# Attention, mixture of experts and gated FFN on one core: token counts one unit later, the last group's factors inside the FFN stage, the silu table loaded early

## The chip, the cores and the metric

One core of a Trainium2 chip runs the whole program. The metric is device microseconds of one launch; the kernel before took 783.86 us, the median of three runs (782.74 to 785.09). One more execution was taken by the profiler; the rows further down are from it.

## The reference, cut to what matters

Three stages follow each other on 2304 tokens of width 512.

```
attention: q, k, v of (4 batches, 8 heads, 576, 64), 128 random features
  phi(x) = exp(h - max h) / sqrt(128),  h = x_s @ omega.T - |x_s|^2 / 2
  out = phi(q) @ (phi(k).T @ v) / (phi(q) . sum phi(k) + 1e-6)
experts (8, 512 -> 1024 -> 512): each token goes to the expert with the
  largest cosine to its embedding
  out[token] = gate * (relu(x @ w1[e]) @ w2[e])
ffn (512 -> 1536 -> 512):
  out = (silu(x @ w_gate) * (x @ w_val)) @ w_out
```

All inputs and outputs are float32.

## The kernel before, in words

**Precision.** A large product is made of three passes: an operand is split into a high part (a cast on ScalarE, line 92) and a low part (the rest, a subtraction on VectorE or GpSimd, line 93), and high x high, high x low and low x high are summed in PSUM. The helper `hi_lo` writes both parts.

**Attention.** Tokens go in 18 tiles of 128, in two groups of nine. The order of this stage is written by hand. Behind each group a class `Routing` works out logits, softmax, the chosen expert of each token, the gate values, and per batch of 576 tokens how many tokens chose each expert. `counts` sums the one-hot rows over the partitions by a small matmul with ones (line 327), turns the gate values by a transpose (line 331), copies them out on ScalarE (line 333) and stores them by a DMA. Then VectorE finds the expert that most tokens of a batch chose (`dom_i`), the counts of the others (`ext_i`) and their total (`tot_i`, line 351), which all engines load into a register (line 1001) for the branch of line 988.

**Experts.** For each batch `expert` runs the dominant expert on all its tokens: four units of hidden columns (`mm1`, 48 matmuls of 288 columns each: two halves of 128 hidden columns, 24 each), then four output chunks (`mm2`, 48 each). The other experts' tokens follow in the branch "extras". Weights of a unit come by a DMA and `hi_lo`; the first two units' low parts are made on GpSimd. For the third unit of the first expert both instructions of `hi_lo` are pinned (`pinned="both"`, lines 94 to 97). PSUM holds two tiles `two` and one tile `third` for these products; a ReLU on ScalarE (line 888) and a subtraction on VectorE (line 889) empty a tile. After the fourth unit `no_y` writes zeros over the output sums `y_g` with 12 ScalarE copies (line 1009). Hooks, keyed by batch and step, put other work between the units: `routing_end` (rest of `Routing` for the second group) stands behind the first unit of the first expert.

**FFN.** Products of 2x2 blocks are done with seven multiplications in place of eight (`PRODUCTS`), so the tokens' activations need seven factors for each of three groups of 768 tokens. `split_y` writes them from `y_g`: `put` is a `hi_lo`, `sub` a subtraction on VectorE (line 965). The last group's `split_y` begins behind the last expert's third output chunk and the rest of it is written at the end of the expert stage. Then, for 12 column blocks and three groups, `tokens` does the seven products (line 1109), empties `a`, `b`, `c` in PSUM (lines 1074 to 1099), applies silu (line 1077), and stores the hidden block to DRAM. `beside` puts the weights' conversion and their seven factors (`seven`) between the products. `out_ahead` fetches a pair of output weight blocks with two DMAs and converts them from 64-bit words (`words`: one ScalarE and six VectorE instructions, the first two pinned). The last stage multiplies hidden blocks by output weights (line 1180).

**What sets the order.** Outside attention, a planner at build time orders each engine's instructions. It takes an instruction when its costs say that its operands are there, and of several the one traced first. `keep_in_program_order` pins an instruction behind the one that was traced just before it on its engine; later ones may still pass it.

Of the kernel before, what the change touches and what calls it, by code (L numbers as in the profile page):

```python
# [10 lines left out]
F32 = mybir.dt.float32  # L11
# [3 lines left out]
AF = mybir.ActivationFunctionType  # L15
# [13 lines left out]
def attention_moe_ffn_kernel(  # L29
# [4 lines left out]
    nc = tc.nc  # L34
# [8 lines left out]
    NF = w64.shape[0]  # L43
# [185 lines left out]
    class Routing:  # L229
# [94 lines left out]
        def counts(self):  # L324
            g = self.g
            p = bank(2, E)
            nc.tensor.matmul(p, ones, self.oc, start=True, stop=True)
            cnt = self.small("cnt", 2, E)
            nc.vector.tensor_copy(cnt, p)
            p = bank(128)  # L330
            nc.tensor.transpose(p[:PT * E, :], self.gt.rearrange("p i e -> p (i e)"), ident)
            gt_t = rt.tile([PT * E, 128], F32, name="gt_t")
            nc.scalar.copy(gt_t, p[:PT * E, :])
            nc.sync.dma_start(out=gts[g], in_=gt_t)
            yield
            cm = self.small("cm", 2)
            dom = self.small("dom", 2, E)
            fst = first_max(cm, dom, cnt, 2, "c")
            nc.vector.tensor_copy(dom_i[:, 2 * g:2 * g + 2], fst[0:1, :])
            yield  # L340
            nc.vector.scalar_tensor_tensor(
                out=cnt, in0=dom, scalar=0.5, in1=cnt, op0=ALU.is_lt, op1=ALU.mult
            )
            c1 = cnt[0:1].rearrange("p j e -> p (j e)")
            nc.vector.tensor_copy(ext_i[:, 2 * g * E:2 * (g + 1) * E], c1)
            nc.vector.tensor_reduce(out=tot[:, g:g + 1], in_=c1, axis=AX.X, op=ALU.add)
            if g == NP - 1:
                nc.vector.tensor_tensor(
                    out=tot[:, 0:1], in0=tot[:, 0:1], in1=tot[:, 1:2], op=ALU.add
                )  # L350
                nc.vector.tensor_copy(tot_i, tot[:, 0:1])
# [491 lines left out]
    with ExitStack() as p2:  # L843
# [104 lines left out]
        def split_y(g):  # L948

            y = y_g[g]  # L950
            if g == 0:
                parts_at[g] = in_x[:14]
            elif g == 1:
                parts_at[g] = in_x[14:] + over_y()
            else:
                late["odd"] = over_y()
                parts_at[g] = [late["odd"].pop() for _ in range(2)] + in_h
            b11, b12 = y[:, 0:2, 0:GB], y[:, 0:2, GB:]
            b21, b22 = y[:, 2:4, 0:GB], y[:, 2:4, GB:]

            def put(q, src):
                hi_lo(factor(g, q, 0), factor(g, q, 1), src, pinned=q == 0)

            def sub(out, x, y):
                nc.vector.tensor_tensor(out=out, in0=x, in1=y, op=ALU.subtract)  # L965

            put(0, b11)
            sub(b11, b12, b11)
            yield
            put(1, b21)  # L970
            put(2, b22)
            sub(b12, b22, b12)
            sub(b22, b22, b11)
            sub(b21, b21, b22)
            put(3, b11)
            put(4, b22)
            put(5, b12)
            put(6, b21)

        xs = {0: first}  # L980
# [35 lines left out]
        def near_extras():  # L1016
            ahead(1)
            xs[1].fetch()
            for eng, ins in late["mark"].items():
                with tc.issue_after(ins.ins):  # L1020
                    tc.mark_branch_hint_location("extras", "LikelyTaken", engines=[eng])

        todo = {
            (0, 0): routing_end, (0, NU - 1): no_y,
            (0, NU + NC - 2): near_extras, (0, NU + NC - 1): extras,
            (2, 0): lambda: weights_ahead(0), (2, NU - 1): lambda: list(split_y(0)),
            (3, 0): lambda: weights_ahead(1), (3, NU - 1): lambda: list(split_y(1)),
            (3, NU + 1): lambda: list(seven(0)), (3, NU + 2): lambda: next(last),
        }
        for bt in range(B):  # L1030
            hooks = {u: go for (b, u), go in todo.items() if b == bt}
            if 0 < bt < LAST:
                hooks[NU + NC - 2] = lambda: ahead(bt + 1)
            expert(xs[bt], bt > 0, hooks)
        next(last, None)
        late["odd"] += over_y()

    late["t"], late["n"] = wpool, 2
    banked.close()
# [16 lines left out]
    with ExitStack() as p3:  # L1056
        sp = p3.enter_context(tc.tile_pool(name="sp", bufs=2, reuse_waits="tile"))
        fps = p3.enter_context(tc.tile_pool(name="fps", bufs=2, space=PSUM, reuse_waits="tile"))


        for k, n in (("b", 2), ("c", 2)):
            fps.tile([128, GB], F32, tag=k, name=k, bufs=n)

        def tokens(f, g):

            bank_of = {
                k: fps.tile([128, GB], F32, tag=k, name=k, bufs=4 if k == "a" else 2)
                for k in "abc"
            }
            c22 = sp.tile([128, GB], F32, tag="c22", name="c22")  # L1070
            cc = sp.tile([128, 2, GB], F32, tag="cc", name="cc", bufs=4)

            def add(out, k):
                nc.vector.tensor_tensor(out=out, in0=bank_of[k], in1=out, op=ALU.add)  # L1074

            def silu(x):
                nc.scalar.activation(out=x, in_=x, func=AF.Silu)  # L1077

            def last_product():
                nc.vector.tensor_tensor(out=cc[:, 0], in0=bank_of["a"], in1=cc[:, 0], op=ALU.mult)  # L1080
                nc.gpsimd.tensor_tensor(out=cc[:, 1], in0=c22, in1=cc[:, 1], op=ALU.mult)  # L1081
                nc.sync.dma_start(
                    out=hds[f][:, g * GW:(g + 1) * GW], in_=cc.rearrange("p a n -> p (a n)")
                )

            def second():
                add(cc[:, 0], "c")
                silu(cc[:, 0])

            def sixth():  # L1090
                add(c22, "a")
                add(cc[:, 1], "b")
                silu(cc[:, 1])

            after = (
                lambda: nc.scalar.copy(cc[:, 0], bank_of["a"]),
                second,
                lambda: nc.scalar.copy(cc[:, 1], bank_of["a"]),  # L1098
                lambda: nc.scalar.copy(c22, bank_of["b"]),
                lambda: None,  # L1100
                sixth,
                last_product,
            )
            begun = set()
            for (wq, xq, k), go in zip(PRODUCTS, after):
                n = 0
                for c in range(2):
                    for a, x in HALVES:
                        nc.tensor.matmul(  # L1109
                            bank_of[k], wq_at(f, wq, a)[:, c * 128:(c + 1) * 128],  # L1110
                            factor(g, xq, x)[:, c],
                            start=(k not in begun), stop=(n == 5), skip_group_check=True,
                        )
                        begun.add(k)
                        n += 1
                go()
                yield

        def beside(n):

            m, k = divmod(n, 3)
            f = 2 * m + k
            yield
            if m == NF // 2:
                out_weights(0)
            elif k == 0 and 0 < m < NF // 2 - 1:
                weights_ahead(f + 1)
            elif k == 1:
                yield from seven(f)
                yield  # L1130
                if f + 1 < NF:
                    weights_ahead(f + 1)
                else:
                    out_ahead(4)
            elif k == 2 and f < NF:
                yield
                yield
                yield from seven(f)
                if f == NF // 2:
                    late["two"] = wpool.tile([128, 2, 2, DM], F32, tag="wp", name="wo32")  # L1140
                if f in (NF // 2, NF // 2 + 2):
                    out_ahead(f - NF // 2, late["two"][:, (f - NF // 2) // 2])
                elif f == NF - 2:
                    weights_ahead(f + 1)
            elif k == 2:
                yield
                out_ahead(6)

        todo = [(f, g) for f in range(NF) for g in range(NG)]
        alone = NG * (NF - 2) - 1  # L1150
        todo = (
            [todo[0:2], todo[2:3]] + [todo[i:i + 2] for i in range(3, alone, 2)]
            + [todo[alone:alone + 1]] + [todo[i:i + 2] for i in range(alone + 1, len(todo), 2)]
        )
        for n, items in enumerate(todo):
            both = [tokens(*at) for at in items]
            also = beside(n)
            for _ in PRODUCTS:
                for t in both:
                    next(t)  # L1160
                next(also, None)
            for _ in also:
                pass

    with ExitStack() as p4:
# [25 lines left out]
        for t0 in range(0, NTI, 8):  # L1191
            n = min(8, NTI - t0)
            ps = [ops.tile([128, DM], F32, tag="o", name="o_ps") for _ in range(n)]
            if n == 8:
                for f in range(NF):
                    if t0 == 0:
                        if f not in wos:
                            out_weights(f)
                        if f in (4, 6):
                            out_ahead(f + 4)  # L1200
                    h = hidden(f, t0, n, n_h % 3, 1024)
                    n_h += 1
# [77 lines left out]
```

## Time and profile before

| | |
|---|---|
| median of three runs | 783.86 us (782.74 to 785.09) |
| the profiled execution | 782.92 us |
| its span, first to last instruction | 780.6 us |
| mean granted TensorE clock | 0.994 |
| TensorE busy | 759.8 us, 97% of the span |
| VectorE, ScalarE, GpSimd busy | 505.1, 361.6, 154.4 us |

Times in the rows are microseconds from the span's start. PE is TensorE, DVE VectorE, ACT ScalarE, POOL GpSimd. A row of the timeline gives start, duration, engine, line, operation, the tiles written and read, how many instructions were merged, and in brackets the idle time before and whose end ended it.

### The profile page before, as it was taken

The numbers are of one execution on the slowest core, as the hardware profiler recorded it, in microseconds if no ns is written. First come the engines' busy times: TensorE is split into PE (matmuls) and PEld (weight loads), VectorE is DVE, ScalarE is ACT, GpSimd is POOL, SyncE is SP. The second block draws the span as 40 slices with busy tenths as digits, with TensorE's granted clock in tenths as the row PEclk, the third lists the DMA queues.
The fourth block names the chain that finished last, engine by engine and source line by source line (L and its number), as shares of the span: only waits on it lengthen the run. The fifth ranks groups of instructions, "written<-read, shape, count | busy, mean of one in ns | idle before, by whom it ended". The sixth has DMA issues, their size and how long they took to land.

```text
span 780.6 us, 14723 instructions
## 1 busy us (share of the span) xinstructions
PE 759.8 (97%) x5860; PEld 711.2 (91%) x5861; DVE 505.1 (65%) x878; ACT 361.6 (46%) x788; POOL 154.4 (20%) x201
## 2 busy tenths in 40 slices
PE   9999889979999999999999999999999999999997
PEld 8878777879999999999999999999999988888886
DVE  5788999563343676786686776898887885212220
ACT  5888568562231352342554454444544642141231
POOL 4864344200002305132111211211211110000000
PEclk9999999999999999999999999999999999999999
DMA  8644642033333323420132232234322573353233
GB/s 285 211 146 155 209 149 98 32 95 110 75 107 135 97 92 126 98 80 1 41 115 95 112 117 95 107 124 148 121 108 100 168 253 108 94 202 109 81 101 115
DMA packets 33908, 94.02 MB, mean 120 GB/s; under 512 B 4240, under 2 KB 8352, under 8 KB 33832
## 3 DMA queue, kind: packets, MB, share of 16 engines
q1 hardware_dynamic: 33672, 92.99, 35.5%
q8 instruction: 47, 0.77, 0.4%
q14 instruction: 29, 0.24, 0.1%
q10 hardware_dynamic: 160, 0.02, 0.0%
HBM read 74.05 MB, written 18.95 MB: 119 GB/s over the span
## 4 chain that ended last, share of the span: by engine, by line
PE 69%; DVE 2%; DMA 1%; ACT 1%; issue 0%; POOL 0%; SPq 0%; ACTq 0%; DVEq 0%; POOLq 0%
PE o_ps L1180 19%; PE a L1109 18%; PE b L1109 9%; PE two L882 7%; PE two L901 5%; PE third L901 5%; PE c L1109 4%; PE third L882 2%; DMA raw<-in_w_dram 1%; POOL y_g L928 0%; DVE xp L93 0%; DVE y_g L965 0%; DVE cc L1074 0%; DVE h_all L93 0%; DVE t L913 0%
## 5 line engine op out<-in xcount | busy, mean ns | idle before, releaser
L1180 PE MATMUL o_ps<-xp 128*128 128x512 f32 x648 | 147.4, 389 | 0.4 <-DVE cc L1080 0.4
L1180 PEld LDWEIGHTS o_ps<-xp 128*128 128x128 f32 x648 | 121.5, 188 | 26.0 <-DVE cc L1080 0.8
L502 ACT ACTIVATE ph<-two,bias 128x128 f32<-128x128 f32 x288 | 78.5, 388 | 28.8 <-DVE bias L493 23.0
L93 DVE TENSOR_TENSOR xp<-h,xp 128x1024 fp32r<-128x1024 f32 (+1 forms) x36 | 34.4, 959 | 88.2 <-ACT xp L92 87.7
L1081 POOL TENSOR_TENSOR cc<-c,cc 128x384 f32<-128x384 f32 x36 | 40.6, 1130 | 227.1 <-ACT cc L1077 204.6
L882 PE MATMUL two<-xp,wp 128*128 128x288 f32 x576 | 81.1, 299 | 0.6 <-PEq L988 0.4
L882 PEld LDWEIGHTS two<-xp,wp 128*128 128x128 f32 x576 | 78.7, 191 | 0.9 <-issue 0.9
L92 ACT CAST xp<-h 128x1024 fp32r<-128x1024 f32 (+1 forms) x36 | 30.1, 838 | 89.9 <-PE o_ps L1180 76.1
L928 POOL TENSOR_TENSOR y_g<-y_g,t 128x192 f32<-128x192 f32 (+3 forms) x29 | 37.3, 1307 | 174.1 <-DVE t L913 174.1
L92 ACT CAST wp<-raw 128x1024 fp32r<-128x1024 f32 x32 | 33.6, 1049 | 58.3 <-PE two L901 29.5
L1077 ACT ACTIVATE cc<-cc 128x384 f32<-128x384 f32 x72 | 37.2, 524 | 47.1 <-DVE cc L1074 47.0
L901 PE MATMUL third<-h_all,wp 128*128 128x288 f32 x384 | 52.8, 296 | 0.0
L901 PE MATMUL two<-h_all,wp 128*128 128x288 f32 x384 | 52.2, 296 | 0.0
L901 PEld LDWEIGHTS third<-h_all,wp 128*128 128x128 f32 x384 | 51.7, 189 | 0.0
L901 PEld LDWEIGHTS two<-h_all,wp 128*128 128x128 f32 x384 | 51.5, 189 | 0.0
L485 DVE TENSOR_REDUCE mx<-two 128x8 f32<-128x1024 f32 x36 | 43.9, 1219 | 7.6 <-PE two L475 7.4
L93 DVE TENSOR_TENSOR wp<-raw,wp 128x1024 fp32r<-128x1024 f32 x30 | 39.9, 1329 | 7.0 <-ACT wp L92 6.7
L1109 PE MATMUL a<-xp,over_y 128*128 128x384 f32 x216 | 43.4, 335 | 0.0
L1109 PE MATMUL a<-xp,wh 128*128 128x384 f32 x144 | 37.2, 339 | 1.2 <-ACT cc L1098 0.7
L1109 PEld LDWEIGHTS a<-xp,over_y 128*128 128x128 f32 x216 | 38.3, 188 | 0.0
L889 DVE SCALAR_TENSOR_TENSOR h_all<-two,h_all 128x576 fp32r<-128x576 f32 x24 | 18.1, 755 | 23.1 <-ACT h_all L888 23.1
L888 ACT ACTIVATE h_all<-two 128x576 fp32r<-128x576 f32 x24 | 15.5, 653 | 35.5 <-PE two L882 35.5
(210 smaller groups left out, 1525.9 us busy)
## 6 DMA issues: line engine op xcount, KB each, us to landing
raw<-in_w_dram SPq DMA_DIRECT2D x68, 512.0 KB, 3.9
hds<-cc SPq DMA_DIRECT2D x36, 384.0 KB, 2.3
h<-hds SPq DMA_DIRECT2D x24, 512.0 KB, 3.6
q<-in_qx_dram SPq DMA_DIRECT2D x18, 512.0 KB, 3.8
k<-in_kx_dram SPq DMA_DIRECT2D x14, 512.0 KB, 4.3
v<-in_vx_dram SPq DMA_DIRECT2D x18, 276.0 KB, 4.1
out_dram<-o SPq DMA_DIRECT2D x18, 256.0 KB, 2.9
h<-hds SPq DMA_DIRECT2D x12, 128.0 KB, 2.2
```

The lines of the kernel that those rows point to most:

```text
L92: go = nc.scalar.copy(hi, src)
L93: low = lo_eng.tensor_tensor(out=lo, in0=src, in1=hi.bitcast(F32), op=ALU.subtract)
L485: nc.vector.tensor_reduce(out=mx.rearrange("p (c a) -> p a c", a=2), in_=p.rearrange("p a (h m) -> p a h m", m=M), axis=AX.X, op=ALU.max,)
L502: nc.scalar.activation(out=ph[:, h, :], in_=p[:, h % 2, h // 2 * M:(h // 2 + 1) * M], func=AF.Exp, bias=bias[:, h:h + 1],)
L882: nc.tensor.matmul(ps[:, j], w[:, a, c, f * 128:(f + 1) * 128], xv[:, c, b, j * HB:(j + 1) * HB], start=(c == 0 and n == 0), stop=(c == NC ...
L889: nc.vector.scalar_tensor_tensor(out=h2[:, 1], in0=ps, scalar=0.0, in1=h2[:, 0].bitcast(F32), op0=ALU.max, op1=ALU.subtract,)
L901: late["mark"][ENG.PE] = nc.tensor.matmul(ps[:, j], w[:, a, f, :], h[:, b, j * HB:(j + 1) * HB], start=(f == 0 and n == 0), stop=(f == len ...
L928: nc.gpsimd.tensor_tensor(out=yv, in0=yv, in1=t, op=ALU.add)
L1077: nc.scalar.activation(out=x, in_=x, func=AF.Silu)
L1081: nc.gpsimd.tensor_tensor(out=cc[:, 1], in0=c22, in1=cc[:, 1], op=ALU.mult)
L1109: nc.tensor.matmul(bank_of[k], wq_at(f, wq, a)[:, c * 128:(c + 1) * 128], factor(g, xq, x)[:, c], start=(k not in begun), stop=(n == 5), s ...
L1180: nc.tensor.matmul(p, h[:, x, i * 128:(i + 1) * 128], wos[f][:, a], start=(f == 0 and k == 0), stop=(f == NF - 1 and k == 2),)
```

## The change

The counts of the second group are traced behind the second unit of the first expert rather than the first, and their matmul is pinned. The last group's factors, all but the first, are written in steps between the first FFN products, rather than at the end of the expert stage. A one-column silu stands behind the last group's first factor, in the last expert. The fetch and conversion of output weight blocks 6 and 7 go from the last step of the FFN loop to the second step of the output stage.

```diff
@@ counts
-            nc.tensor.matmul(p, ones, self.oc, start=True, stop=True)
+            go = nc.tensor.matmul(p, ones, self.oc, start=True, stop=True)
+            if g == NP - 1:
+                tc.keep_in_program_order(go)
@@ split_y
             put(1, b21)
+            yield
             put(2, b22)
             sub(b12, b22, b12)
             sub(b22, b22, b11)
+            yield
+            put(4, b22)
             sub(b21, b21, b22)
+            yield
             put(3, b11)
-            put(4, b22)
+            yield
             put(5, b12)
+            yield
             put(6, b21)
@@ hooks
+        def split_begin():
+            next(last)
+            silu_set = tp.tile([128, 1], F32, tag="silu", name="silu_set")
+            tc.keep_in_program_order(nc.scalar.activation(out=silu_set, in_=zero, func=AF.Silu))
+
         todo = {
-            (0, 0): routing_end, (0, NU - 1): no_y,
+            (0, 1): routing_end, (0, NU - 1): no_y,
...
-            (3, NU + 1): lambda: list(seven(0)), (3, NU + 2): lambda: next(last),
+            (3, NU + 1): lambda: list(seven(0)), (3, NU + 2): split_begin,
...
-        next(last, None)
-        late["odd"] += over_y()
+        late["last"] = last
@@ beside
-            if m == NF // 2:
+            if n == 0:
+                yield from late["last"]
+                late["odd"] += over_y()
+            elif m == NF // 2:
                 out_weights(0)
...
-            elif k == 2:
-                yield
-                out_ahead(6)
@@ output stage
                         if f not in wos:
                             out_weights(f)
-                        if f in (4, 6):
+                        if f == 1:
+                            out_ahead(6)
+                        elif f in (4, 6):
                             out_ahead(f + 4)
```

## Rows read from the trace of the kernel before

**Rows 1.** The page's first part: busy time, share of the span, instructions.

```profile
PE 759.8 (97%) x5860; PEld 711.2 (91%) x5861; DVE 505.1 (65%) x878; ACT 361.6 (46%) x788; POOL 154.4 (20%) x201
```

**Rows 2.** Waits of TensorE: who waited for whom, total, times, longest.

```profile
PE one L327 <- DVE oc L302: 4.0, 1, 4.0
...
PE a L1109 <- ACT cc L1098: 0.7, 1, 0.7
...
PE a L1109 <- ACT cc L1096: 0.5, 1, 0.5
...
PE o_ps L1180 <- DVE cc L1080: 0.4, 1, 0.4
```

**Rows 3.** Timeline of TensorE around the counts.

```profile
159.78 3.36 PE L882 MATMUL two<-xp,wp 128*128 128x288 f32 x24
...
167.45 0.37 PE L327 MATMUL one<-oc,ones 128*128 128x16 f32 x2 [4.03 <-DVE oc L302]
167.66 1.16 PE L882 MATMUL two<-xp,wp 128*128 128x288 f32 x4
...
169.58 3.84 PE L882 MATMUL two<-xp,wp 128*128 128x288 f32 x22
173.26 0.27 PE L331 MATMUL one<-ident,gt 128*72 128x128 f32 x1
```

**Rows 4.** Timeline of ScalarE in the same stretch.

```profile
156.94 7.43 ACT L1009 COPY y_g<-zero 128x192 f32<-128x192 f32 x12
164.27 1.05 ACT L92 CAST wp<-raw 128x1024 fp32r<-128x1024 f32 x1
...
165.76 0.65 ACT L888 ACTIVATE h_all<-two 128x576 fp32r<-128x576 f32 x1
166.29 1.05 ACT L92 CAST wp<-raw 128x1024 fp32r<-128x1024 f32 x1
...
174.34 0.25 ACT L333 COPY gt_t<-one 72x128 f32<-72x128 f32 x1
```

**Rows 5.** Timeline of VectorE in the same stretch.

```profile
165.82 1.21 DVE L93 TENSOR_TENSOR wp<-raw,wp 128x1024 fp32r<-128x1024 f32 x1
166.96 0.35 DVE L302 TENSOR_TENSOR oc<-oc,oh 64x8 f32<-64x8 f32 x2
...
168.01 0.75 DVE L889 SCALAR_TENSOR_TENSOR h_all<-two,h_all 128x576 fp32r<-128x576 f32 x1
...
170.60 0.23 DVE L311 TENSOR_TENSOR gt<-oh,se 128x72 f32<-128x72 f32 x1
```

**Rows 6.** Windows: length, busy by engine, granted clock (PEclk), DMA share, GB/s.

```profile
168.50:169.50 1.00, 1.00 (x6) 1.00 (x5) 1.00 (x2) 0.00 (x0) 0.00 (x0) 0.50 0.68 258
...
368.00:374.00 6.00, 5.36 (x29) 5.04 (x29) 5.38 (x8) 4.46 (x8) 0.00 (x0) 1.00 0.00 0
```

**Rows 7.** Chain that ended last: one piece of a unit, start, us.

```profile
218.45 6.40 PE two L882 x48
```

**Rows 8.** Timeline of TensorE in the first FFN products.

```profile
362.33 0.62 PE L1109 MATMUL a<-xp,wh 128*128 128x384 f32 x2
...
368.19 0.62 PE L1109 MATMUL a<-xp,wh 128*128 128x384 f32 x2 [0.50 <-ACT cc L1096]
...
374.27 0.61 PE L1109 MATMUL a<-xp,wh 128*128 128x384 f32 x2 [0.72 <-ACT cc L1098]
```

**Rows 9.** Timeline of ScalarE there.

```profile
366.19 1.57 ACT L92 CAST h_all<-y_g 128x768 fp32r<-128x768 f32 x2 [7.04 <-POOL y_g L928]
...
371.62 1.28 ACT L1077 ACT_TABLE_LOAD   x1
...
373.75 0.46 ACT L1098 COPY cc<-a 128x384 f32<-128x384 f32 x1
```

**Rows 10.** Timeline of VectorE there: the last group's last factor, low part.

```profile
375.36 0.96 DVE L93 TENSOR_TENSOR h_all<-y_g,h_all 128x768 fp32r<-128x768 f32 x1 [1.97 <-ACT h_all L92]
```

**Rows 11.** Timeline of ScalarE at the end of the FFN loop.

```profile
629.17 1.13 ACT L780 ACTIVATE cv_t<-raw 128x1024 f32<-128x1024 f32 x1 [2.57 <-DMA raw<-in_w_dram]
```

## The prediction

> **What bounds the kernel.** I read the page's busy times first: TensorE is busy 759.8 of 780.6 us [rows 1], so only 20.8 us are not its work, and every edit can be priced by the TensorE wait that it touches. The list of TensorE's waits comes second. The largest is the counts' matmul on VectorE's one-hot sums, 4.0 us once; the first FFN products wait 0.7 and 0.5 us for ScalarE copies; the output stage's start waits 0.4 us [rows 2]. These four, 5.6 us, are all that the edits aim at. Third come the timelines of the engines at those places, which decide whether a wait is the last one or only the one that is named.
>
> **Counts behind the second unit.** TensorE's timeline shows what stands where: the second unit's last 24 products start at 159.78, and after 4.03 us of idleness, from 163.4, come the counts at 167.45, then products of units three and four [rows 3]. So the counts' matmul stands behind the second unit already; its new place in the program is the one that the planner gave it, and its pin binds nothing more. What changes is what is traced behind it.
>
> Would TensorE have had work in the 4.03 us? ScalarE's timeline says no. Twelve copies of zeros hold it from 156.94 to 164.37 (7.43 us); only then comes a weight cast at 164.27, the ReLU of the second unit at 165.76, another cast at 166.29 [rows 4]. The third unit's cast is pinned behind that ReLU, so the one at 166.29 is the third unit's and the one at 164.27 the fourth's. The third unit's high weights are thus there at 166.29 + 1.05 = 167.34, the fourth's low ones at 165.82 + 1.21 = 167.03 [rows 4, 5]. The counts' operand ends at 166.96 + 0.35 = 167.31 [rows 5]. Two waits end within 0.03 us; taking the named one away gives almost nothing. The zeros are not touched by the change.
>
> The move also costs. `routing_end` issues the softmax, gates and counts on VectorE, an exponential and the gate copy on ScalarE, two TensorE instructions, one small DMA on SP's queue and a register load on every engine; it is now traced before the third unit's fetch. That unit's pinned cast then stands behind the gate copy (line 333), and its pinned low part behind the last counting instruction. Before, the cast ran at 166.29 and the gate copy only at 174.34 [rows 4]. So the third unit's weights turn from the first ones ready into the last. Queued behind the cast on ScalarE are later weight casts, which nobody needs before the output chunks; SP's weight fetches are released with the low parts and have several us to spare; GpSimd has no part in it.
>
> TensorE then begins with the fourth unit. Why did it not do so before, with the high weights there at 164.27 + 1.05 = 165.32 [rows 4]? I read it so: the free PSUM tile is kept for the third unit, and the fourth gets the other `two` tile when VectorE has emptied it, at 168.01 + 0.75 = 168.76 [rows 5]. So the restart is at 168.76, not 167.66 [rows 3]: 1.1 us lost. Does a second hole follow? The gates end at 170.60 + 0.23 = 170.83, behind a low-weight subtraction of 1.21 us that is no longer ahead of them, so about 169.6 [rows 5]. With the transpose (0.27), the copy (0.25), the cast (1.05) and the subtraction (1.21) the third unit is ready at about 169.6 + 2.8 + some waits = 173, if the transpose stands well forward in TensorE's queue. The fourth unit's 24 products last from 168.76 to about 173.6: 30 products stand in the three rows from 167.66 to 173.26 (4, 4 and 22) and take 5.6 us [rows 3], where 48 take 6.40 at full rate, 0.133 each [rows 7], so 30 cost 1.6 us extra and 24 take 24 x 0.133 + 1.6 = 4.8. It just fits: no second hole. I take **+1.1 us**. Bounds: if the fourth unit gets the free tile after all, its products run from 167.03 rather than 167.66, with four done earlier at half rate, some 1.0 us: at most 1.6 us gained; if the transpose stands behind all 24, the second hole below, up to +4.8.
>
> The 1.6 us are the clock: in the stretch after the idleness the granted clock is 0.50, the level of 1.2 GHz, with 6 products in a microsecond [rows 6]. After the short waits of 0.50 and 0.72 us it stayed at 1.00, 2.4 GHz [rows 6, 8].
> The Trainium skill (TensorE: Matmul & The Clock Gate, "What's actually happening") says that the gate follows how busy the array has been recently, idle meaning half rate. By that rule a true removal of the 4.0 us would bring 5.6 us rather than 4.0; the trace agrees with the fall, and no run yet shows the return without the gap.
>
> **Silu table.** The load takes 1.28 us at 371.62, and a copy at 373.75 behind it releases the product at 374.27, after 0.72 us of idleness [rows 8, 9]. In the last expert ScalarE idles 7.04 us before 366.19 [rows 9], which hides the load and a one-column silu; if that cover were gone, the cast at 366.19 would come 1.3 us later. With the load away the copy is 1.28 us earlier, more than the 0.72 us of wait: **-0.7**. Next in line would be VectorE's additions, which are not waited for in this stretch. Bounds -0.7 and 0.
>
> **Factors between the products.** Six `put`s (a cast and a subtraction each) and three `sub`s move, no DMA. They can't start earlier: the first two casts wait for GpSimd's last sum, to 366.19 [rows 9]. What can change is that the copy that ends the 0.50 us wait [rows 8] goes ahead of the two casts (1.57 us). But the planner takes what is ready first by its costs; it had those casts first with the copy's operand long there, and the trace order decides only a tie. I take **0**; the lower bound is -0.5. Upwards: the last low part ends at 375.36 + 0.96 = 376.3 [rows 10], and the third group needs it last, after 2 x 42 + 36 products of 0.185 us each (29 in 5.36 us [rows 6]) from 362.33 on [rows 8], near 384. That is 7 us of cover, yet VectorE also makes the second block's factors behind them; +1.0 bounds it.
>
> **Output weights.** Two DMAs on SP, one ScalarE and six VectorE instructions move past the loop's end. The ScalarE one ran at 629.17 when its data landed [rows 11], and would be ready at the same moment in the new place; its pin is now behind the first hidden block's cast. Bounds: the start's 0.4 us wait [rows 2] gone, or doubled. I take **0**.
>
> **Sum.** +1.1 - 0.7 + 0 + 0 = +0.4. The profiled execution took 782.92 us (span 780.6 and 2.3 around it), which gives 783.3; the median of the runs lies 0.94 higher: **784.3 us**.
>
> **The rivals.**
> *The counts' wait goes.* If the planner lets TensorE run on behind the second unit, 4.0 us, the 1.6 us of half rate, 0.7 and 0.5 us go: 783.86 - 6.8 = 777.1. For it: the wait has the counts' name. Against: no weights before 165.3, and the zeros in front of them. Chance 0.12.
> *The free tile goes to the fourth unit.* -1.6 - 0.7 = -2.3: 781.6. Against it is the order before, where that unit with its weights ready stood behind the third. Chance 0.13.
> *The change does nothing at the counts.* The pinned cast floats in some way back to its place; the wait stays, the table's 0.7 goes: 783.2. Chance 0.13.
> *A second hole (slower).* The gates' transpose stands behind all 24 products of the fourth unit. They end at 173.6; transpose 0.27, copy 0.25 and cast 1.05 with their hand-overs bring the third unit's high weights to 175.4, or 176.4 with another weight cast ahead, and the low ones stop TensorE 0.3 us more. 2.1 to 3.1 us on top of 1.1, so about +3.7, and more if the clock falls again: 783.86 + 3.7 - 0.7 = 786.9, up to 788.5. It decides from where the transpose comes later than some 18 products into the fourth unit. For it: before, the transpose stood 26 products behind the restart [rows 3]. Chance 0.20.
> The forecast keeps 0.42, its own range 783.0 to 785.8.
>
> **How the numbers follow.** 0.3% is 2.35 us, about what a measurement here can tell from no change: faster is below 781.5, slower above 786.2. Faster holds the first rival and a third of the second, 0.16; slower most of the last and a tail of the forecast, 0.20; the rest, 0.64, is no change. The range leaves out the first rival and the far tail of the last: 780.2 to 788.0.
>
> **What would show it.** Right: a TensorE gap from about 163.4 to 168 or later in front of the counts or the fourth unit, a cast of weights behind line 333's copy, the table load near 356, no wait for line 1098. Wrong: TensorE's units running on at full clock past 163.4, or a second gap near 174, or new waits for factors near 377 to 384.

## The result, and the profile after

The changed kernel took 789.74 us, the median of six runs (788.9 to 791.84), against 783.8 us for the kernel before in the same comparison. The ratio is 1.0083, with a 95% interval of 1.006 to 1.0106: slower, and outside the predicted range. The forecast of 784.3 us was wrong. All times are medians of fast runs; one run of x2_counts_only, an experiment further down, was in a slow state with 1232.03 us and is left out.

The profiled execution took 789.36 us, its span 787.3. TensorE has the same 5860 instructions as in [rows 1] and is busy 2.8 us longer; the span grew by 6.7:

```profile
PE 762.6 (97%) x5860; PEld 713.7 (91%) x5861; DVE 506.3 (64%) x878; ACT 361.8 (46%) x789; POOL 153.4 (19%) x201
```

Where the 6.7 us lie is seen from four starting times: TensorE's of the router's products (line 257), of the first output chunk (line 901, now 903) and of the first FFN product, and ScalarE's of the copy of the last output.

| stretch | before | after | |
|---|---|---|---|
| start to the router's products | 158.38 | 158.72 | +0.34 |
| router's products to first output chunk ("the counts' stretch") | 23.76 | 29.54 | **+5.78** |
| first output chunk to first FFN product | 180.19 | 181.72 | +1.53 |
| first FFN product to last copy | 414.42 | 413.43 | -0.99 |
| last copy to the end | 3.85 | 3.89 | +0.04 |

The list of TensorE's waits, after, against [rows 2] (who waited for whom: total, times, longest):

```profile
PE one L327 <- DVE oc L302: 4.0, 1, 4.0
PE two L884 <- ACT wp L92: 2.5, 1, 2.5
...
PE one L333 <- DVE cand L161: 1.9, 1, 1.9
PE two L884 <- issue: 1.5, 1, 1.5
...
PE o_ps L1191 <- DVE cc L1091: 0.4, 1, 0.4
...
PE o_ps L1191 <- DVE cc L1085: 0.3, 1, 0.3
```

The counts' wait stays whole; two new ones of 1.9 and 2.5 us stand behind it. The waits of 0.7 and 0.5 us on the FFN's copies are gone. In TensorE's timeline the three waits follow each other, where [rows 3] have one:

```profile
163.41 0.35 PE L269 MATMUL one<-ident,lt 16*128 16x16 f32 x3
167.79 0.37 PE L327 MATMUL one<-oc,ones 128*128 128x16 f32 x2 [4.03 <-DVE oc L302]
170.11 0.40 PE L333 MATMUL one<-ident,gt 128*72 128x128 f32 x1 [1.95 <-DVE cand L161]
173.01 1.33 PE L884 MATMUL two<-xp,wp 128*128 128x288 f32 x4 [2.51 <-ACT wp L92]
...
188.26 6.56 PE L903 MATMUL third<-h_all,wp 128*128 128x288 f32 x48
...
217.43 5.46 PE L884 MATMUL two<-xp,wp 128*128 128x288 f32 x39 [1.54 <-issue]
```

Between 163.4 and 173.0 not one product of units three or four runs. The reason is on ScalarE and VectorE. ScalarE's rows that answer to [rows 4]:

```profile
164.61 1.05 ACT L92 CAST wp<-raw 128x1024 fp32r<-128x1024 f32 x1
...
170.54 0.26 ACT L335 COPY gt_t<-one 72x128 f32<-72x128 f32 x1 [3.65 <-PE one L333]
171.92 1.04 ACT L92 CAST wp<-raw 128x1024 fp32r<-128x1024 f32 x1 [1.11 <-DVE tot_i L353]
```

The cast that ran at 166.29 now stands at 171.92, behind the gate copy. What releases it is `tot_i`, the total of the counts: its load into a register of ScalarE, at 201.5 in the kernel before, is the last that the counting issues there, and the pin ties the cast to it (engine queue, operation: duration ns, when):

```profile
L1008 ACTq TENSOR_LOAD <-tot_i x1: 513/513/513, 171.3 to 171.3; - x1
```

VectorE's rows for [rows 5] show that the fourth unit, meanwhile, had all it needed:

```profile
166.17 1.21 DVE L93 TENSOR_TENSOR wp<-raw,wp 128x1024 fp32r<-128x1024 f32 x1
...
168.35 0.75 DVE L891 SCALAR_TENSOR_TENSOR h_all<-two,h_all 128x576 fp32r<-128x576 f32 x1
...
172.99 1.23 DVE L93 TENSOR_TENSOR wp<-raw,wp 128x1024 fp32r<-128x1024 f32 x1 [1.70 <-ACT wp L92]
```

Its high weights are there at 164.61 + 1.05 = 165.66, the low ones at 167.38, the second `two` tile is empty at 168.35 + 0.75 = 169.10. TensorE starts at 173.01, with the third unit. The granted clock (windows: from and to, length, busy time of PE, PEld, DVE, ACT and POOL, clock, DMA share, GB/s) stays at the 1.2 GHz level long after that start:

```profile
176.00:178.00 2.00, 2.00 (x11) 2.00 (x10) 0.00 (x0) 0.09 (x1) 0.00 (x0) 0.50 0.52 195
178.00:180.00 2.00, 2.00 (x15) 2.00 (x15) 1.01 (x1) 0.95 (x1) 0.00 (x0) 0.90 0.02 4
```

So the +5.78 us are two new waits, 1.95 + 2.51 = 4.46, and a remainder of 1.32 us, products at half rate: over the whole stretch, before and after, TensorE is busy 19.73 and 21.05 us with 136 instructions each, at a mean granted clock of 0.93 and 0.83.

```profile
158.38:182.14 23.76, 19.73 (x136) 19.48 (x135) 14.41 (x47) 13.12 (x20) 0.00 (x0) 0.93 0.25 76
...
158.72:188.26 29.54, 21.05 (x136) 20.47 (x135) 14.56 (x46) 13.32 (x20) 0.00 (x0) 0.83 0.21 64
```

In the FFN the table load stands ahead of the first product (369.98), and the copy of line 1107 now waits for TensorE and no longer TensorE for it:

```profile
363.78 1.28 ACT L1033 ACT_TABLE_LOAD   x1
...
371.33 0.48 ACT L1107 COPY cc<-a 128x384 f32<-128x384 f32 x1 [4.50 <-PE a L1120]
```

### The profile page after: what moved, and what is told of

It is laid out like the page before. It is cut to its first block, busy times and chain, and to the rows that moved or that the text cites. A ratio compares the mean times of both kernels' runs of the same rounds, so it can differ in the third digit from the quotient of the medians.

```text
span 787.3 us, 14727 instructions
## 1 busy us (share of the span) xinstructions
PE 762.6 (97%) x5860; PEld 713.7 (91%) x5861; DVE 506.3 (64%) x878; ACT 361.8 (46%) x789; POOL 153.4 (19%) x201
## 4 chain that ended last, share of the span: by engine, by line
PE 70%; DVE 1%; DMA 1%; issue 1%; ACT 0%; ACTq 0%; DVEq 0%
PE o_ps L1191 19%; PE a L1120 18%; PE b L1120 9%; PE two L884 7%; PE two L903 5%; PE third L903 5%; PE c L1120 5%; PE third L884 2%; DMA h<-hds 1%; DVE xp L93 0%; DVE cc L1085 0%; DVE cv_t L798 0%; ACT xp L92 0%; DVE raw L795 0%; ACT o L1198 0%
```

## The experiments

The theory after the result: the loss comes from the pinned weights of the third unit, which the counts' new place makes late, and from a fourth unit that doesn't pass the third. Rivals: the place of the counts costs by itself; the FFN edits cost; the zeros on ScalarE, not the counts, hold TensorE. Each kernel was compared with the kernel before on the same chip; the two stretches are those of one profiled execution each.

| kernel | us | ratio to before, 95% interval | counts' stretch | FFN stretch |
|---|---|---|---|---|
| after | 789.74 | 1.0083 [1.006, 1.0106] | 29.54 | 413.43 |
| x1_counts_back | 784.75 | 0.9998 [0.9987, 1.0008] | 24.95 | 414.49 |
| x2_counts_only | 790.44 | 1.0067 [1.0047, 1.0087] | 29.54 | 412.96 |
| x3_weights_first | 785.21 | 0.9996 [0.9984, 1.0009] | 23.76 | 414.56 |
| x4_zeros_gpsimd | 778.31 | 0.9918 [0.9897, 0.9939] | 19.65 | 413.62 |
| x5_all_early | 778.57 | 0.9927 [0.9904, 0.9951] | 18.18 | 414.74 |
| x6_third_tile | 786.48 | 1.0035 [1.0017, 1.0053] | 23.50 | 414.18 |
| x7_early_no_ffn | 778.2 | 0.9929 [0.9904, 0.9955] | 18.18 | 416.16 |
| x8_weights_early | 780.86 | 0.9955 [0.9939, 0.9972] | 22.00 | 413.42 |
| x9_after_unpinned | 778.13 | 0.9936 [0.9911, 0.996] | 19.58 | 413.87 |
| x10_before_unpinned | 778.08 | 0.9928 [0.9902, 0.9953] | 19.61 | 413.00 |
| x11_unpinned_zeros_gpsimd | 788.28 | 1.0062 [1.0038, 1.0086] | 27.83 | 415.37 |
| x12_fourth_on_third | 786.83 | 1.0029 [1.0012, 1.0046] | 25.73 | 413.95 |

### Which edit costs: x1 and x2

x1 is the kernel after with the counts put back; x2 is the kernel before with the same lines edited the other way, the counts moved and nothing else.

```diff
-            go = nc.tensor.matmul(p, ones, self.oc, start=True, stop=True)
-            if g == NP - 1:
-                tc.keep_in_program_order(go)
+            nc.tensor.matmul(p, ones, self.oc, start=True, stop=True)
...
-            (0, 1): routing_end, (0, NU - 1): no_y,
+            (0, 0): routing_end, (0, NU - 1): no_y,
```

> The changed kernel with the counts' hook back behind the first unit and without their pin; the other three edits stay. Theory 1 (the slowdown is the third unit's weights, cast behind the counting work): the first expert's first output chunk starts near 182 to 182.5 us as before, rather than at 188.3; the FFN stage stays about 1.0 us shorter; the kernel ends 0.5 to 1.5 us below the kernel before. Theory 2 (the factors between the products or the moved output weights cost part of the 6.7 us): it stays 1 us or more above the kernel before. If the 1.5 us gap of TensorE behind the branch is part of the FFN edits, it is there again; if it follows the counts, it is gone.

> The kernel before with only the counts' hook and pin changed. Theory 1: 5.8 us between the end of the first unit's pair and the first output chunk (TensorE idle 4.0, 2.0 and 2.5 us, and some 25 products at half rate), in all 5.5 to 7.5 us above the kernel before. Theory 2: less than 4 us above.

x1 stands at the kernel before (its profile has a stretch 1.2 us longer, which its times don't show), x2 at the kernel after. The whole loss belongs to the move of the counts, and the FFN edits together are worth nothing that can be measured; the 1.0 us that x1 was to keep in the FFN is not in its profile (414.49 us, 414.42 before). x2 repeats the two new waits to the hundredth:

```profile
171.75 0.40 PE L333 MATMUL one<-ident,gt 128*72 128x128 f32 x1 [1.95 <-DVE cand L161]
174.66 1.33 PE L884 MATMUL two<-xp,wp 128*128 128x288 f32 x4 [2.51 <-ACT wp L92]
```

### The third unit's weights ahead of the counts: x3 and x8

x3 keeps the counts behind the second unit, but traces the third unit's fetch and conversion first. x8 does the same in the kernel before, behind the first unit, so that the cast is pinned ahead of the zeros.

```diff
+        def third_then_counts():
+            xs[0].fetch()
+            routing_end()
...
x3, against the kernel after:
-            (0, 1): routing_end, (0, NU - 1): no_y,
+            (0, 1): third_then_counts, (0, NU - 1): no_y,
x8, against the kernel before:
-            (0, 0): routing_end, (0, NU - 1): no_y,
+            (0, 0): third_then_counts, (0, NU - 1): no_y,
```

> The changed kernel, but the third unit's weights are fetched and cast (in the program's order) ahead of the counting work, at the same hook behind the second unit; counts and pin stay where the change put them. Theory 1 (what costs is that the pinned cast and subtraction stand behind the counting work): the cast goes back to about 166.3 us, the stall to one wait of 4.0 us, the first output chunk to 182 to 182.5; the kernel ends 0.5 to 1.5 us below the kernel before. Theory 3 (the counts' own place or pin on TensorE costs): it stays 5 to 7 us above.

> The kernel before with only the third unit's fetch moved ahead of the counting work, behind the first unit; the zeros stay on ScalarE. If weights, not the counts, keep TensorE idle before 167, its products of the third unit run on at 163.4 behind the transposes, ahead of the counts, and the 4.0 us wait is gone though the zeros are where they were; a later wait for the second unit's ReLU, which the zeros hold to 166 or 167, may stand in its place for 1 to 2 us: 3 to 5 us gained. If the counts' operand sets the wait, nothing changes.

In x3 one line, in the same hook ahead of the counts, takes back all of the loss: the stretch is 23.76 us, that of the kernel before. So not the place of the counts but what it does to these weights costs 5.8 us. The 0.5 to 1.5 us below the kernel before, expected of x1 and x3 from the FFN edits, came in neither. In x8 the counts wait for nothing. What is left is a wait for the tile `third`, which the third unit's second half needs: the second unit's ReLU that reads it is still behind the zeros (166.71), and VectorE's subtraction that empties it stands behind a weight subtraction of 1.23 us and ends at 169.70:

```profile
163.75 0.35 PE L269 MATMUL one<-ident,lt 16*128 16x16 f32 x3
164.03 3.33 PE L882 MATMUL two<-xp,wp 128*128 128x288 f32 x23
167.20 0.29 PE L327 MATMUL one<-oc,ones 128*128 128x16 f32 x2
...
169.75 4.85 PE L882 MATMUL third<-xp,wp 128*128 128x288 f32 x24 [2.27 <-DVE h_all L889]
```

### The zeros on GpSimd: x4, x5 and x7

x4 is the kernel before with the zeros written by GpSimd. x5 and x7 add an early fetch of the third unit and put the counts behind the third, x5 with the FFN edits, x7 without.

```diff
x4, x7 (before), x5 (after):
-                    nc.scalar.copy(y, zero.to_broadcast([128, y.shape[1]]))
+                    nc.gpsimd.memset(y, 0.0)
...
x5 and x7 besides:
+            (0, 0): xs[0].fetch, (0, 2): routing_end, (0, NU - 1): no_y,
```

> The kernel before with the twelve copies of zeros on GpSimd instead of ScalarE. If the counts' wait of 4.0 us hides a second wait for weights that the zeros hold back, as the prediction said, taking the zeros off ScalarE brings the third unit's cast to about 164 and lets TensorE begin it by about 165: the wait falls from 4.0 to 1.0 to 2.5 us, and 1.5 to 4 us are gained in all with the clock. If the counts' operand alone sets the wait, the wait stays at 3 us or more and under 1 us is gained.

> The changed kernel with three things more: the third unit's weights fetched in the program's order behind the first unit, the counts behind the third unit, the zeros on GpSimd. Theory 1: no wait for weights or counts is left between 163 and 180 us, the clock stays up, the section from the logits' transposes to the first output chunk falls from 19.1 us (before) to 12.8 to 13.5; against the zeros on GpSimd alone 1.4 us more. If the FFN edits are worth nothing, as the counts put back showed, it stands level with the next kernel but one within 1 us: 6 to 8 us below the kernel before.

> The kernel before with the third unit's weights fetched in the program's order behind the first unit, the counts behind the third unit and the zeros on GpSimd; the FFN edits left out. Theory 1: the same section of 12.8 to 13.5 us, 6 to 8 us below the kernel before. What it stands above the kernel with the FFN edits is what these are worth: 0 to 1 us.

x4 gains 0.8% with the counts untouched, so the largest wait of the list was not the counts' alone: the zeros held the weights until the same moment. A smaller wait for those weights is left, and then the counts come behind 42 products:

```profile
164.86 0.79 PE L882 MATMUL two<-xp,wp 128*128 128x288 f32 x4 [1.39 <-ACT wp L92]
165.49 0.69 PE L882 MATMUL third<-xp,wp 128*128 128x288 f32 x4
166.02 4.69 PE L882 MATMUL two<-xp,wp 128*128 128x288 f32 x34
170.55 0.29 PE L327 MATMUL one<-oc,ones 128*128 128x16 f32 x2
```

x5 and x7 have no wait in the stretch: 18.18 us. Their expectation of 12.8 to 13.5 us from the logits' transposes can't be read as it was meant, since those transposes now stand 15 products later; from the router's products on, the gain is 23.76 - 18.18 = 5.58 us, the 4.03 of the wait and 1.55 of half rate. That their stretch is 1.47 us shorter than that of x4 does not show in the times. The two agree, 0.9927 and 0.9929, though x7 shows the largest FFN waits of all:

```profile
PE o_ps L1180 <- DVE cc L1080: 1.5, 1, 1.5
...
PE a L1109 <- ACT cc L1098: 0.7, 1, 0.7
...
PE a L1109 <- ACT cc L1096: 0.5, 1, 0.5
```

### May the fourth unit pass the third: x6 and x12

Both are the kernel after with the two PSUM tiles dealt out differently. In x6 the third unit's first half takes the tile `third` (its second half has it already). In x12 the third unit takes both tiles `two`, and the fourth unit's first half the tile `third`.

```diff
x6:
-        return third() if n_banks[0] % 3 == 0 else banks()
+        return third() if n_banks[0] % 3 == 0 or n_banks[0] == 5 else banks()
x12:
-        return third() if n_banks[0] % 3 == 0 else banks()
+        return third() if n_banks[0] % 3 == 0 and n_banks[0] != 6 or n_banks[0] == 7 else banks()
```

> The changed kernel, but both halves of the third unit use the PSUM tile third, so that the fourth unit is the next in line for the tiles two. Theory 4 (PSUM tiles are handed out in the order of the program, so the fourth unit stood still in the changed kernel until the third, with its late weights, had taken its tile): the fourth unit's products start ahead of the counts, near 167.5 us, the two later holes of 2.0 and 2.5 us close, and the section from the transposes to the first output chunk falls from 24.9 to 18 to 20.5 us. Theory 5 (the fourth unit waits for something else, such as its own weights): the first product after the transposes stays behind 172 us.

```profile
165.51 0.80 PE L884 MATMUL two<-xp,wp 128*128 128x288 f32 x4 [1.95 <-ACT wp L92]
...
170.93 0.44 PE L327 MATMUL one<-oc,ones 128*128 128x16 f32 x2
...
182.02 0.79 PE L903 MATMUL two<-h_all,wp 128*128 128x288 f32 x4 [1.85 <-ACT wp L92]
```

In x6 the fourth unit starts at 165.51, as soon as its weights are there, and the counts' wait is gone. In the kernel after it did not, with the same weights at the same time. The holes did not close as expected. From the transposes to the first output chunk it takes 18.81 us, inside the forecast, but that flatters: the third unit, both halves on one tile, runs its second half only behind the first output products (from 186.31 on), waits such as the one of 1.85 us follow, and up to the second expert's first product only 1.84 us come back (53.91 us from the router's products, against 55.75 after and 49.97 before). x6 leaves open whether a tile that is merely emptied early would have done, since the `two` that it frees had stood empty for long. x12 asks that: the tile `third` is emptied at about the same time (168.44) as the `two` that the fourth unit has in the kernel after (169.10).

> The kernel after, with two tiles exchanged: the third unit's second half takes a tile two and the fourth unit's first half the tile third, which is emptied at 168.44 us, 0.7 us earlier than the second tile two that the fourth unit has in the kernel after. The third unit's first half keeps its tile. Theory (tiles of one pool are handed out in the order of the program, and only that holds the fourth unit back): its 24 products start right behind the counts, at about 168.4, 4.6 us earlier than any product in the kernel after. Then the blind prediction's picture comes true, in the form of its slower rival, since the gates' transpose stands behind the 24 products: they end at about 173.2, the gate copy follows, then cast and subtraction, and the third unit starts at about 175.5 to 176.5 behind a hole of 2 to 3 us. The stretch from the router's products to the first output chunk is 26.5 to 28 us, the time 786.5 to 788.5, ratio 1.003 to 1.006. Rival (the fourth unit is held by something else, its weights or the counts): no product of it before 173, the stretch 29.5, the ratio 1.008.

```profile
167.62 0.58 PE L327 MATMUL one<-oc,ones 128*128 128x16 f32 x2 [4.02 <-DVE oc L302]
168.32 5.11 PE L884 MATMUL third<-xp,wp 128*128 128x288 f32 x24
173.27 0.27 PE L333 MATMUL one<-ident,gt 128*72 128x128 f32 x1
173.30 6.62 PE L884 MATMUL two<-xp,wp 128*128 128x288 f32 x48
181.06 3.39 PE L884 MATMUL two<-xp,wp 128*128 128x288 f32 x24 [1.15 <-DVE h_all L891]
```

The fourth unit starts at 168.32, right behind the counts, and its 24 products last to 173.4: what the prediction had for the kernel after (168.76 to 173.6), to half a microsecond. The part of the expectation on a second hole was wrong: the cast ran ahead of the gate copy here, at 171.70, and the third unit follows at 173.30 without a gap. The stretch is 25.73 us, +1.97 against the kernel before and not +5.78; 1.15 of the 1.97 is a wait for a tile that the exchange brought.

### The pin itself: x9, x10 and x11

x9 is the kernel after and x10 the kernel before, each without the pin of the third unit's weights; x11 is x10 with the zeros on GpSimd as in x4.

```diff
-            hi_lo(w[:, 0], w[:, 1], raw, low, pinned="both" if first else False)
+            hi_lo(w[:, 0], w[:, 1], raw, low, pinned=False)
```

> The kernel after, with the cast and the subtraction of the third unit's weights no longer pinned; counts behind the second unit as in the change. Theory: the new place of the counts costs 5.8 us only through this pin, which puts the third unit's cast behind the gate copy and the register load; the fourth unit then waits for a PSUM tile behind the third. Without the pin the cast finds a place before the 12 copies of zeros, no wait of 4.0, 1.95 or 2.51 us is left, and from the router's products to the first output chunk it takes about 18.2 us, as in the kernel with zeros on GpSimd and an early third fetch, against 29.5 us in the kernel after: the whole at 778.3 to 780.5 us, ratio to before 0.993 to 0.996 (the two casts that come earlier may hold the end of attention for up to 2.1 us). Rival: the counts' place itself costs (its products, copy and chain of VectorE in the middle of the units), or the tiles alone: the time stays at 788 to 790, ratio 1.005 to 1.008.

> The kernel before, with the pin of the third unit's weights taken away and nothing else. If the weights and not the counts' place decide, the wait of 4.0 us goes here too, with the counts traced where they were: same section as in the run before it, 778 to 780.5 us, ratio 0.993 to 0.996, and the two runs agree within 0.2%. Rival: the wait belongs to the counts' place; then this one keeps a wait of 4 us for line 302 and stays at 783 to 785.

> The kernel before, without the pin and with the zeros written by GpSimd. If both edits remove the same wait, the two together bring no more than the better one: 777 to 779 us, ratio 0.992 to 0.994. If they remove different waits they add up: 774 to 776.

x9 and x10 agree with each other and beat both kernels. In x9 ScalarE casts the third and the fourth unit's weights when their data land, before the zeros:

```profile
150.99 1.05 ACT L92 CAST wp<-raw 128x1024 fp32r<-128x1024 f32 x1 [2.59 <-DMA raw<-in_w_dram]
...
156.92 1.05 ACT L92 CAST wp<-raw 128x1024 fp32r<-128x1024 f32 x1 [1.18 <-DMA raw<-in_w_dram]
...
159.42 7.44 ACT L1016 COPY y_g<-zero 128x192 f32<-128x192 f32 x12
```

TensorE then runs through, in the same kernel that waited 4.03, 1.95 and 2.51 us with the pin:

```profile
161.30 3.48 PE L884 MATMUL two<-xp,wp 128*128 128x288 f32 x25
164.71 0.35 PE L269 MATMUL one<-ident,lt 16*128 16x16 f32 x3
164.99 3.31 PE L884 MATMUL two<-xp,wp 128*128 128x288 f32 x23
...
170.95 0.29 PE L327 MATMUL one<-oc,ones 128*128 128x16 f32 x2
...
178.33 6.56 PE L903 MATMUL third<-h_all,wp 128*128 128x288 f32 x48
```

The stretch is 19.58 us, not the expected 18.2: 0.88 us is a new wait of the router's products, whose last operand stands behind the earlier casts. The zeros are harmless here, with 7.44 us on ScalarE as before; they cost only while weights stood behind them.

x11 fell outside both of its expectations: two edits that gain 0.8% and 0.7% alone lose 0.6% together. TensorE waits 6.99 us for the router's last operand, and VectorE's row says why: a right shift of nine columns takes 6.91 us.

```profile
155.51 6.91 DVE L178 TENSOR_SCALAR ny<-ss 128x9 int32<-128x9 int32 x1 [0.73 <-ACT x L597]
```

It ends at 162.42, where GpSimd's 12 memsets end, at 162.39:

```profile
155.61 6.78 POOL L1009 MEMSET y_g<- 128x192 f32 x12
```

In the kernel before, the same shift starts at 153.93, takes 0.85 us, and ends at 154.78, where a subtraction on GpSimd ends too (152.34 + 2.40 = 154.74); in x4 the two ends are 154.80 and 154.77, and the memsets come later. In x10 it takes 0.19 us and ends at 156.40, the subtraction at 156.37. That VectorE's shift waits for GpSimd is thus read from the ends: in all fourteen kernels it ends 0.02 to 0.04 us behind GpSimd's subtraction, or in x11 behind its memsets. No run was made for it alone.
The Trainium skill (SBUF — State Buffer, "SBUF: two separate sides") says that the two engines share a pair of ports as an exclusive lock, that VectorE takes part in it with an operation in a two-port mode, or with one that has two inputs in SBUF against a GpSimd operation that reads SBUF, that the lock is held for a whole instruction, and that the loser blocks fully. Which mode the shift ran in no run shows. The trace agrees on the blocking, but it lasted over twelve GpSimd instructions here (6.78 us), not one.

## Why the prediction was wrong

**What bounds the kernel: right.** TensorE's waits set the time. That two waits ended together, the counts' operand and the weights behind 7.43 us of zeros, is read from the rows and shown from the weights' side: x4, x8 and x10 give the weights earlier, leave the counts where they are, and the 4.03 us go (1.39 us for weights are left in x4, 2.27 for a tile in x8). No run gave the counts' operand earlier and left the weights late. The counts' wait stayed whole in the kernel after, as forecast. The new pin on the counts binds nothing: without it the built program has the same order on every engine.

**The third unit's weights turn from the first ones into the last: right in time, wrong in the anchor.** I had them ready at about 173; the high ones were there at 172.96, the low ones at 174.22. But what held the cast was not the gate copy. I had counted the register load among what the move issues, and overlooked that it is the instruction to which the pin then ties the cast. x12 shows it: there the cast runs at 171.70, behind `tot_i`, and the gate copy only at 174.02.

**The step that failed: "TensorE then begins with the fourth unit", at 168.76, "1.1 us lost".** The fourth unit, with weights at 167.38 and a tile `two` empty at 169.10, stood still until the third had started at 173.01. The sign of it was in [rows 4]: before, the fourth unit had its high weights at 165.32 and did not start ahead of the third. I read that as a tile kept free for the third and took it that the next tile to come empty would serve the fourth. x12 shows that this is what failed: the fourth unit on a tile of another tag, emptied 0.7 us earlier, starts at 168.32, its 24 products cover the third unit's conversion, and the loss is +1.97 us, near the +1.1. What fits both x6 and x12 is that tiles of one tag are handed out in the order of the program: the fourth unit's comes only after the third's first write, though it is empty before. That it is this order and not the planner's costs is inferred, since no run leaves the third unit on `two` and gives the fourth a `two` that has long been empty. In place of +1.1 us stand two holes, 1.95 + 2.51 = 4.46, and 1.32 us of half rate. "It just fits: no second hole" was right in x12, where the fourth unit could start.

**The rival of a second hole** had the sign and, at 786.9 to 788.5, most of the size, with a chance of 0.20. Its mechanism did not occur: the transpose stood at 170.11, right behind the counts, with no product of the fourth unit ahead. Priced without those 24 products, the same rows give the third unit at 173 against 167.66 in [rows 3], some 5.3 us. So its nearness to the result is luck. Its support was miscounted too: by the 4, 4 and 22 products of the trace the transpose stood 30 products behind the restart, not 26.

**Silu table, factors, output weights: -0.7, 0 and 0.** The table's wait of 0.72 us went, as did the 0.50, and the output stage's start got a second small wait (0.28 us). None of it can be measured: the FFN stretch is 414.17 us in the mean of the seven kernels with the edits and 414.14 in the seven without, which differ by up to 3.2 us among themselves. x2 and x4 lost both waits without the edits, by the planner's other choices. My -0.7 took one row for a fixed cost where the planner's order moves more.

**The clock.** By the prediction 4.03 us of idleness cost 1.6 us of half rate on top. x5 and x7, without the wait and with a granted clock of 1.00 over the whole stretch, give 5.58 - 4.03 = 1.55. By the rule named there (the Trainium skill, TensorE: Matmul & The Clock Gate, "What's actually happening") the sum was 5.6, and this trace now agrees.

**Left over.** The +1.53 us behind the first output chunk are one gap of 1.54, "issue", at 215.9 to 217.4, behind the branch. x2 and x12 have it too (1.37 us each); x1, x3, x8, x10 and x11 have one of 0.3 to 0.4, the others none. The three have the counting work traced ahead of the third unit's pinned weights, but so has x6 without the gap; its cause stays open.

## What to carry to other kernels

Where two waits end together, the list names only the later one: before moving the named work, look at what its neighbours in the queue would start with. A pin ties an instruction to whatever is traced just before it, so every move of other work past that point moves the pinned one too; here taking the pin away (x10, 0.9928) or moving the zeros (x4, 0.9918) each gave what the change was after, and both together lost it again. And, by what x6 and x12 suggest, a later unit covers an earlier one's wait only if its tile is not handed out behind the earlier one's.

## What was not expected of the hardware

The half clock outlasted short gaps: after waits of 4.03, 1.95 and 2.51 us, with two small matmuls between, the granted clock was still 0.50 at 176 to 178 us, three and more microseconds into the unbroken products that follow 173.01. In x12, with the one wait of 4.02 us, it was at 1.00 again from 173 on, where the products had started at 168.32. In x4 a single wait of 1.39 us left it at 1.00; in x8 a single one of 2.27 us was followed by 0.50 at 169.7 to 171 and 0.52 at 171 to 173. A nine-column VectorE instruction took 0.19, 0.85 or 6.91 us, by what GpSimd did beside it.
